# Packing eight heads of 48 into three full blocks of 128 rows instead of four padded ones, with the work replanned around it

## The chip, the core and the metric

The kernel runs on one core of one Trainium2 chip. The core has five instruction queues that run beside each other: PE (matmuls and transposes into the eight PSUM banks), DVE (elementwise, reads PSUM and SBUF), ACT (elementwise with functions such as exp and ln, reads PSUM and SBUF), POOL (elementwise, SBUF only here) and SP (issues the loads and stores). Each runs its instructions in the order in which they were written; semaphores hold an instruction until what it needs is done. The metric is the device time of one execution in microseconds (us); the number for a kernel is the median of its runs.

## What is computed

Two stages. The first is a recurrence over 768 tokens with a state of 48x48 for each of 4 batches x 8 heads; the second mixes tokens within a batch.

```python
B, H, S, D = 4, 8, 768, 48
for t in range(S):
    cur = einsum('bhd,bhe->bhde', u * k[t], v[t])
    y[t] = einsum('bhd,bhde->bhe', r[t], state + cur)
    state = w[t][..., None] * state + einsum('bhd,bhe->bhde', k[t], v[t])
x = y.transpose(0, 2, 1, 3).reshape(B, S, 384)
W = einsum('bsd,btd->bst', x @ w_q, x @ w_k) / 8
out = maximum(einsum('bst,btd->bsd', W, x), 0) @ w_out
```

`r`, `k`, `v`, `w` are float32 of 4x8x768x48 (4.7 MB each), the output is 4.7 MB; inside, bfloat16 operands and float32 sums are used.

## The kernel before

The recurrence is done in chunks of 128 tokens: with `L` the running sum of ln w inside a chunk, `RT = r*exp(L)` and `KT = k*exp(-L)`, the scores of a chunk are `KT^T RT` under a triangular mask, and the state carries what lies before the chunk. A unit is 256 tokens (two chunks) of one batch, so there are 12 units (`n`), three in a batch. For each unit the steps are, by their keys in the code:

- loads `wg`, `kg`, `rg`, `vg` (SP); casts to bfloat16 `k16`, `r16`, `v16` (POOL, a few on ACT); `ln` (ACT, L403);
- `cw`: sums of ln w by matmul with a triangular matrix `CM`; `ep`, `en`: the two exponentials (ACT, L444 and L451);
- `kT`, `rT`: transposes on PE, so that the 48 values of a head lie on the rows; `ks`, `qT`, `RT` (DVE) and `KT` (POOL or DVE) read them from PSUM;
- `vp`/`VB`: a matmul with a permutation `PM` puts v into the order of tokens that the transposes give, and a copy takes it to SBUF; `dps`/`dd`/`Vd`: the bonus term with `u`;
- `A`: scores, one matmul for each head; `AM`: mask (DVE, L592); `kb`/`kd`/`sn`/`SB`: next state;
- `yi`, `ya`: output from state and from scores; `X`: sum with `Vd` (DVE, L724); `xt`/`XT`: transpose; `qk`/`QK`: the projections.

After the third unit of a batch come `T`/`TS` (k-projection times x), and for each unit `mx` (PE), `rl` into `MX` (DVE or ACT), `fp` (times `w_out`), `os` (copy to SBUF) and the store.

The 48 values of a head are padded to 64 rows: two heads fill a block of 128 rows, and a chunk has four blocks (`NP`), so `ks`, `qT`, `RT`, `KT` and `en` are 2 x 512 = 1024 columns wide for a unit. A matmul over one head uses a tile of 64 rows of the array; two heads side by side use both.

`k` and `r` are loaded in runs of four tokens (768 bytes, L232) except in unit 0, `w` and `v` in runs of two (384 bytes, L227), and `v` of the last batch by four DMAs in runs of one token (192 bytes, `vw`, L238), which spares that batch `v16` and `vp`. Units 0 and 11 do `ep`, `en`, `RT`, `KT`, `Vd`, `kb`, `kd` by chunk rather than by unit; unit 11 also `X`, `xt`, `XT` and the projections.

What sets the order: the steps are recorded in a plan, and three tables written in the file, `ORDER`, `WAYS` and `BANKS`, say in which order they are issued, on which engine a step with a choice runs (`A` ACT, `D` DVE, `P` POOL; `E`, `e`, `c` for forms of PE work) and in which PSUM bank a result lies. Nothing is scheduled at run time: an engine that waits holds up all that is behind it.

Of the kernel before, what the change touches and what calls it, by code (L numbers as in the profile page):

```python
# [23 lines left out]
class Buf:  # L24
    def __init__(self, kind, tile=None):
        self.kind = kind
        self.tile = tile
        self.filler = None
        self.before = None
        self.bank = None  # L30


class Plan:

    ENGINE = dict(E="E", e="E", c="E", A="A", D="D", d="D", P="P", S="S", T="S", N="N")

# [4 lines left out]
    def add(self, key, ways, fn, after=(), buf=None, reads=(), cols=0, mode=0, behind=None,  # L43
            half=-1, more=None):
        s = dict(key=key, ways=ways, way=ways[0], fn=fn, after=list(after), buf=buf,
                 reads=list(reads), cols=cols, mode=mode, behind=behind, half=half,
                 more=more or {}, i=len(self.steps), fills=False, out=False)
        if buf is not None:
            if buf.filler is None:
                buf.filler = s  # L50
                s["fills"] = True
                if buf.tile is None:
                    self.banks.append(buf)
                elif behind is None and buf.before is not None:
                    s["behind"] = buf.before.filler
            elif behind is None:
                s["behind"] = buf.filler
        self.steps.append(s)
        return s

    def order(self):
# [7 lines left out]
        assert all((way[("yv",) + k[1:]] == "E") == (w == "A") for k, w in way.items() if k[0] == "X")  # L69
# [4 lines left out]
        for i in ORDER:  # L74
            s = self.steps[i]
            assert s["way"] == "N" or all(x["out"] for x in s["after"]), s["key"]
            if s["buf"] is not None and s["buf"].kind == "x":
                s["buf"].kind = "s" if s["way"] == "E" else "w"
            s["out"] = True
            done.append(s)  # L80
# [38 lines left out]
]  # L119
WAYS = (  # L120
    "PPDPPDPPDDDDDDPDTTPDDAAPPDPPPADDDEENDEAAPPDdPADEAEENDEAAAPAPPADEDcNDEDAAAAAAAAPADdPAAEAc"
    "cNDEADPPDdPAAeAcENDeDAPPDPPAAeAENDEAAAAAAAAAPPDPPAAEDEENDEAAPPDdPAAeAEENDEAAPPDPPAAEAcND"
    "EDAAADAAAAPPDPPAEAEcNDeAAPPDPPAeAccNDeDAPPDPPPAPPAENDEDADNDEAADDDDAAAAAADDADNNEEEENEEENE"
    "NENENNNNNNEN"
)
BANKS = [
# [7 lines left out]
]  # L134


WARM = 24


@with_exitstack  # L140
def kernel(
# [24 lines left out]
    HW = H * D2  # L166
    N = B * NU

# [33 lines left out]
    if not WHOLE:  # L202
        del RINGS["vw"]
# [702 lines left out]
```

## Time and profile before

| what | value |
|---|---|
| runs | 101.3, 103.6, 104.62 us; median 103.6 |
| span of the profiled execution, first to last instruction | 101.1 us |
| granted clock of PE over the span | 1.000 |
| bytes moved, share of time the DMA queue of SP was busy | 24.68 MB, 86.9% |
| packets | 45165, of which 31576 under 512 bytes |

No time of its own is recorded for the profiled execution beside its span; the span lies 0.2 us below the fastest of the runs and 2.5 us below their median. In the rows further down, an engine's busy time counts overlapping instructions once, while the mean of a group is of single instructions, so count times mean is a little more than the busy time. Matmul rows have modelled ends; the distance from one start to the next says more than a duration.

### The profile page before, as it was taken

What the parts mean: (1) busy time and instruction counts of PE and PEld (TensorE: products, weight loads), DVE (VectorE), ACT (ScalarE), POOL (GpSimd) and SP (SyncE); (2) the same over time, 40 slices, a digit from 0 to 9 for tenths busy, and PEclk for the clock granted to TensorE, in tenths of its full rate; (3) what the DMA queues carried; (4) which work ended last, traced back from release to release, by engine and by line L of the source; (5) the groups of instructions that cost most, each with busy time, mean ns of one, the idle gap of its engine ahead of it and who ended that gap; (6) DMA issues with size and microseconds to landing.
All of it is one profiled execution on the core that took longest, in us unless ns stands there. A gap on an engine that the chain in (4) does not pass through costs nothing.

```text
span 101.1 us, 4474 instructions
## 1 busy us (share of the span) xinstructions
PE 86.8 (86%) x1906; PEld 63.4 (63%) x1909; DVE 80.5 (80%) x134; ACT 80.9 (80%) x134; POOL 68.8 (68%) x82
## 2 busy tenths in 40 slices
PE   5966984989899888999899988999999998999920
PEld 1334553777597556678577875787877667776500
DVE  5423896899999989889999899999997897565520
ACT  5068975999799699599998999989997995735930
POOL 6858964699937764968899749999995897000000
PEclk9999999999999999999999999999999999999999
DMA  1999998999999999999999799999888831007591
GB/s 26 309 324 346 332 317 227 341 261 274 313 306 240 257 205 244 291 329 341 224 323 287 192 343 301 166 155 250 229 233 310 314 141 67 0 0 303 209 366 69
DMA packets 45165, 24.68 MB, mean 244 GB/s; under 512 B 31576, under 2 KB 43992, under 8 KB 45144
## 3 DMA queue, kind: packets, MB, share of 16 engines
q1 hardware_dynamic: 44984, 24.19, 86.9%
q8 instruction: 15, 0.25, 1.0%
q10 hardware_dynamic: 160, 0.20, 0.6%
q14 instruction: 6, 0.05, 0.2%
HBM read 19.66 MB, written 4.72 MB: 241 GB/s over the span
## 4 chain that ended last, share of the span: by engine, by line
PE 34%; ACT 15%; DMA 13%; DVE 12%; SPq 10%; issue 7%; POOL 4%; DVEq 0%; POOLq 0%; ACTq 0%
PE PS L177 34%; DMA vg<-in_v_dram 7%; DMA kg<-in_k_dram 6%; ACT ep L444 6%; SPq L227 5%; ACT en L451 4%; SPq L232 4%; DVE AM L592 3%; DVE X L724 2%; ACT os L275 2%; POOL v L281 2%; DVE ks L281 1%; POOL r L414 1%; DVE RT L513 1%; DVE qT L503 1%
## 5 line engine op out<-in xcount | busy, mean ns | idle before, releaser
L592 DVE TENSOR_TENSOR AM<-PS,US 128x1024 bf16<-128x1024 f32 x24 | 28.7, 1216 | 0.9 <-PE PS L177 0.6
L523 POOL TENSOR_TENSOR KT<-ks,en 128x1024 bf16<-128x1024 bf16 (+1 forms) x10 | 17.4, 1739 | 2.7 <-DVE qT L503 2.0
L572 POOL TENSOR_TENSOR Vd<-VB,dd 128x768 bf16<-128x768 bf16 (+1 forms) x14 | 18.0, 1292 | 1.5 <-ACT dd L275 1.0
L444 ACT ACTIVATE ep<-PS,kp 128x512 bf16<-128x512 f32 (+1 forms) x28 | 16.3, 646 | 0.1
L451 ACT ACTIVATE en<-PS,km 128x1024 bf16<-128x1024 f32 (+1 forms) x14 | 13.9, 1002 | 1.1 <-ACT QK L275 0.8
L724 DVE TENSOR_TENSOR X<-PS,Vd 128x768 bf16<-128x768 f32 (+1 forms) x13 | 11.6, 889 | 2.7 <-POOL Vd L572 1.4
L177 PE MATMUL PS<-wo,MX 128*128 128x384 bf16 x72 | 13.3, 326 | 0.2 <-ACT ep L444 0.2
L177 PEld LDWEIGHTS <-KT 48*128 48x128 bf16 (+1 forms) x312 | 10.3, 94 | 5.1 <-issue 2.6
L177 PE MATMUL PS<-RT,KT 48*128 48x128 bf16 x192 | 9.6, 217 | 1.9 <-POOL KT L523 1.0
L414 POOL CAST k<-kg 128x768 bf16<-128x768 f32 x10 | 8.2, 824 | 3.6 <-DMA kg<-in_k_dram 1.8
L281 DVE COPY ks<-PS 128x1024 bf16<-128x1024 bf16 x11 | 7.6, 689 | 3.7 <-PE PS L177 3.7
L275 ACT COPY os<-PS 128x768 f32<-128x768 f32 (+1 forms) x13 | 8.8, 679 | 1.9 <-PE PS L177 1.6
L414 POOL CAST r<-rg 128x768 bf16<-128x768 f32 x10 | 8.2, 824 | 3.1 <-DMA rg<-in_r_dram 1.9
L513 DVE TENSOR_TENSOR RT<-PS,ep 128x1024 bf16<-128x1024 bf16 (+1 forms) x14 | 8.5, 608 | 2.2 <-ACT ep L444 2.0
L403 ACT ACTIVATE lw<-wg 128x768 bf16<-128x768 f32 x12 | 10.1, 850 | 0.1
L177 PEld LDWEIGHTS <-MX 128*128 128x128 bf16 x72 | 6.4, 97 | 4.3 <-DVE MX L289 0.3
L287 ACT ACTIVATE MX<-PS 128x768 bf16<-128x768 f32 (+1 forms) x11 | 8.2, 758 | 0.9 <-PE PS L177 0.8
L275 ACT CAST VB<-PS 128x768 bf16<-128x768 f32 x9 | 7.3, 806 | 1.8 <-PE PS L177 1.7
L281 POOL CAST v<-vg 128x768 bf16<-128x768 f32 x9 | 7.4, 823 | 1.8 <-DMA vg<-in_v_dram 1.7
L177 PE MATMUL PS<-CM,lw 64*128 64x128 bf16 x192 | 7.9, 217 | 0.7 <-issue 0.4
L656 DVE TENSOR_TENSOR SB<-PS,ep 128x192 bf16<-128x192 f32 x20 | 7.0, 350 | 1.6 <-PE PS L177 1.5
L503 DVE TENSOR_TENSOR qT<-PS,ks 128x1024 bf16<-128x1024 bf16 x12 | 8.2, 681 | 0.0
(82 smaller groups left out, 182.8 us busy)
## 6 DMA issues: line engine op xcount, KB each, us to landing
kg<-in_k_dram SPq DMA_DIRECT2D x12, 384.0 KB, 5.5
wg<-in_w_dram SPq DMA_DIRECT2D x12, 384.0 KB, 6.3
rg<-in_r_dram SPq DMA_DIRECT2D x12, 384.0 KB, 6.4
vg<-in_v_dram SPq DMA_DIRECT2D x9, 384.0 KB, 6.9
out_dram<-os SPq DMA_DIRECT2D x9, 384.0 KB, 3.2
vw<-in_v_dram SPq DMA_DIRECT2D x4, 288.0 KB
out_dram<-os SPq DMA_DIRECT2D x5, 192.0 KB, 2.8
wof<-in_moe_w_out_dram SPq DMA_DIRECT2D x1, 450.0 KB
```

Source lines behind the costliest of these rows:

```text
L177: return nc.tensor.matmul(o, l, rr, start=start, stop=stop, skip_group_check=True, is_transpose=trans)
L275: nc.scalar.copy(o, i)
L281: x.tensor_copy(o, i)
L403: nc.scalar.activation(view(lw.tile, 0, [[64, H], [512, 2], [1, D]]), view(g["wg"].tile, 0, [[D2, H], [D, 2], [1, D]]), ACT.Ln, bias=0.0, ...
L414: op(view(o.tile, 0, [[64, NP], [256, 4], [1, D]]), view(g[src].tile, 0, [[2 * D2, NP], [D, 4], [1, D]]))
L444: nc.scalar.activation(view(ep.tile, cs[0] * NP * EW + off, [[EW, NP * len(cs)], [step, 2], [1, 32]]), view(at(cw), cs[0] * 512 + j * 64, ...
L451: nc.scalar.activation(en.tile[:, ds(cs[0] * 512, w_)], at(cw)[:, ds(cs[0] * 512, w_)], ACT.Exp, bias=km, scale=-1.0)
L513: nc.vector.tensor_tensor(plain(RT.tile, cs, 32), turned(512, cs, True), plain(ep.tile, cs, EW // 4), ALU.mult)
L523: x.tensor_tensor(KT.tile[:, cols], ks.tile[:, cols], en.tile[:, cols], ALU.mult)
L572: (nc.vector if e == "D" else nc.gpsimd).tensor_tensor(Vd.tile[:, cols], VB.tile[:, cols], view(dd.tile, cs[0] * H, [[1, len(cs) * H], [0, ...
L592: AMs[c] = add(("AM", n, c), "D", lambda e, c=c, A=A: nc.vector.tensor_tensor(view(AM[c].tile, 0, [[C, 8], [1, C]]), view(at(A), 0, [[C, 8 ...
L724: nc.vector.tensor_tensor(o, y_, view(Vd.tile, c0 * DM, dims), ALU.add)
```

## The change

Each head's 48 values are cut into 32 and 16. Block 0 holds the 32 of the even heads (four strips of 32 rows), block 2 the 32 of the odd heads, and block 1 in each strip the 16 of an even and the 16 of the odd head beside it. A chunk has three full blocks (`G`) instead of four, and `ks`, `qT`, `KT`, `en` and the data of `RT` are 768 columns wide for a unit instead of 1024. Scores and state products of a head become two accumulated matmuls on tiles of 32 rows (`HEADS`). [...]

```diff
+    G = DM // 128
+    R = D2 // G
-    LONG = tuple(range(1, N))
-    WHOLE = (B - 1,)
+    DIRECT = ()
...
         def f_ln(e):
-            nc.scalar.activation(view(lw.tile, 0, [[64, H], [512, 2], [1, D]]),
-                                 view(g["wg"].tile, 0, [[D2, H], [D, 2], [1, D]]), ACT.Ln,
-                                 bias=0.0, scale=1.0)
+            for o, x in blocks(lw.tile, g["wg"].tile):
+                nc.scalar.activation(o, x, ACT.Ln, bias=0.0, scale=1.0)
...
+        def blocks(o, x):
+            return ((view(o, 0, [[R, NP], [C, 4], [1, R]]),
+                     view(x, 0, [[2 * D2, NP], [D, 4], [1, R]])),
+                    (view(o, 4 * C, [[R // 2, H], [C, 2], [1, R // 2]]),
+                     view(x, R, [[D2, H], [D, 2], [1, R // 2]])))
...
+        eps = add(("ep", n), "A", lambda e: nc.scalar.activation(
+            view(ep.tile, 1, [[EC, 2], [EW, G], [1, C]]),
+            view(at(cw), 0, [[512, 2], [C, G], [1, C]]), ACT.Exp, bias=kp, scale=1.0),
...
+        RTs = add(("RT", n), "D", lambda e: nc.vector.tensor_tensor(
+            view(RT.tile, 0, [[512, 2], [1, DM]]), turned(0),
+            view(ep.tile, 65, [[EW, 2 * G], [-65, 2], [1, 64]]), ALU.mult),
+            [rTs, eps] + fresh("ep"), RT, [kr, ep])
+        def f_RM(e):
+            o, x = (view(RT.tile, y * C, [[512, 2], [1, C]]) for y in (3, 1))
+            if e == "A":
+                nc.scalar.activation(o, x, ACT.Copy, bias=0.0, scale=pm)
+            else:
+                on(e).tensor_scalar_mul(o, x, pm)
+        RMs = add(("RM", n), "PDA", f_RM, [RTs, su["pm"]], RT, [])
...
+        HEADS = (((0, 0, 0, R), (1, 1, 1, R // 2)), ((1, 3, 2, R), (2, 2, 3, R)))
+        As = [wide(), wide()]
-            def f_A(e, c=c, A=A):
-                x = at(A)
-                for hp in range(NP):
-                    for hh in range(2):
-                        mm(x[:, ds(hh * 512 + hp * C, C)],
-                           KT.tile[ds(hh * 64, D), ds((c * NP + hp) * C, C)],
-                           RT.tile[ds(hh * 64, D), ds((c * NP + hp) * C, C)])
+        def f_A(e):
+            for c in pair:
+                for hh in range(2):
+                    for y, (kx, rx, _, n_) in enumerate(HEADS[hh]):
+                        for hp in range(NP):
+                            p = ds(hp * R, n_)
+                            mm(at(As[hp // 2])[:, ds(hp % 2 * 512 + c * 256 + hh * C, C)],
+                               KT.tile[p, ds(c * DM + kx * C, C)],
+                               RT.tile[p, ds(c * 512 + rx * C, C)],
+                               start=(c == 0 and hh == 0 and y == 0), stop=(y == 1))
```

`A` is now one step of 32 matmuls for both chunks of a unit and fills four banks at once; `AM` is split by heads, not by chunk. The output `y` of a unit likewise lies in four banks (`ys = [wide(), wide()]`, two before) and `X` is two passes of 384 columns instead of one of 768. `ln` and the casts of `k` and `r` are two instructions each, `ep` is one instead of two. The next state (`sn`) is written by matmuls into 32 rows at a time. In the build, PE has 2229 matmuls where it had 1909.

All four inputs are loaded by `load` in runs of two tokens (384 bytes); `load_long` and `load_whole` are gone, so the last batch has `v16`, `vp` and `VB` like the others. The treatment of units 0 and 11 by chunk is gone but for `rl`, `fp` and `os` of the last batch. The rings `ep`, `RT`, `KT` and `VB` have three buffers instead of two, `os` nine instead of four. The weights are loaded in one DMA each instead of two. `ORDER`, `WAYS` and `BANKS` are new throughout; a few values of `ORDER` read

```diff
-    38, 15, 441, 301, 32, 18, 649, 644, 22, 539, 645, 2, 3, 26, 25, 0, 401, 581, 4, 5, 34, 33, 23,
+    24, 25, 26, 27, 114, 68, 69, 70, 115, 71, 116, 2, 7, 8, 0, 16, 4, 6, 5, 15, 1, 3, 30, 21,
```

What the tables do shows at three places. The first is DVE at the start of the program, from its first read of transposed data on (`X` and `Vd` of the first units stand further down). Before:

```order
L281 COPY ks_95<-PS 128x1024
L513 TENSOR_TENSOR RT_99<-PS,ep_91 128x512
L503 TENSOR_TENSOR qT_97<-PS,ks_95 128x1024
L513 TENSOR_TENSOR RT_99<-PS,ep_91 128x512
L592 TENSOR_TENSOR AM_0_111<-PS,US 128x1024
L283 TENSOR_SCALAR kd_83<-PS 128x8x48
L281 COPY ks_96<-PS 128x1024
L281 COPY dd_107<-PS 128x16
```

and after:

```order
L480 TENSOR_TENSOR KT_108<-PS,en_99 128x768
L290 MEMSET US 128x128
L290 MEMSET ep_96 128x6
L465 TENSOR_TENSOR RT_105<-PS,ep_96 128x2x384
L475 TENSOR_SCALAR RT_105<-RT_105,pm 128x2x128
L461 TENSOR_TENSOR qT_103<-PS,ks_101 128x768
L540 TENSOR_TENSOR AM_0_120<-PS,US 128x1024
L273 COPY UB<-PS 128x24
L290 MEMSET ep_97 128x6
L540 TENSOR_TENSOR AM_0_122<-PS,US 128x1024
```

`RT` of unit 0 was in two halves and is whole, `RM` (the TENSOR_SCALAR with `pm`) follows it, and both masks of unit 0 stand close together; `ks` of unit 0 has gone to ACT.

The second is DVE at the end, from the last mask on. Before:

```order
L592 TENSOR_TENSOR AM_1_114<-PS,US 128x1024
L724 TENSOR_TENSOR X_126<-PS,Vd_110 128x384 x2
L281 COPY os_81<-PS 128x768
L281 COPY XT_120<-PS 128x384
L281 CAST QK_128<-PS 128x128 x2
L281 CAST TS_130<-PS 128x384
L289 TENSOR_SCALAR MX_122<-PS 128x3x128 x2
L289 TENSOR_SCALAR MX_124<-PS 128x3x128 x2
L281 COPY os_82<-PS 128x384
```

and after:

```order
L540 TENSOR_TENSOR AM_1_123<-PS,US 128x1024
L646 TENSOR_TENSOR X_135<-PS,Vd_118 128x2x192
L646 TENSOR_TENSOR X_135<-PS,Vd_119 128x2x192 x2
L646 TENSOR_TENSOR X_135<-PS,Vd_118 128x2x192
L273 COPY XT_129<-PS 128x768
L281 TENSOR_SCALAR MX_130<-PS 128x768
L273 CAST QK_137<-PS 128x384 x2
L273 CAST TS_139<-PS 128x384
L273 COPY os_86<-PS 128x768
L281 TENSOR_SCALAR MX_132<-PS 128x3x128 x2
L273 COPY os_80<-PS 128x384
L273 COPY os_79<-PS 128x384 x2
```

Units 10 (`Vd_118`) and 11 (`Vd_119`) now end side by side: their four passes of `X` and both projections `QK` come behind the last mask, where before only those of unit 11 did; of the last copies `os`, DVE has three instead of one.

The third is SP where the loads end and the stores begin. Before (`vw` is v of the last batch):

```order
L232 DMA kg_73<-in_k_dram 128x4x192
L227 DMA wg_65<-in_w_dram 128x8x96
L232 DMA rg_69<-in_r_dram 128x4x192
L238 DMA vw_131<-in_v_dram 32x48x48 x4
L849 DMA out_dram<-os_79 128x768
L227 DMA wg_66<-in_w_dram 128x8x96
L232 DMA kg_74<-in_k_dram 128x4x192
L232 DMA rg_70<-in_r_dram 128x4x192
L849 DMA out_dram<-os_80 128x768
```

and after:

```order
L228 DMA kg_73<-in_k_dram 128x8x96
L228 DMA rg_69<-in_r_dram 128x8x96
L228 DMA kg_74<-in_k_dram 128x8x96
L228 DMA rg_70<-in_r_dram 128x8x96
L228 DMA vg_77<-in_v_dram 128x8x96
L228 DMA vg_78<-in_v_dram 128x8x96
L739 DMA out_dram<-os_83 128x768
L739 DMA out_dram<-os_81 128x768
```

The four loads of `vw` are gone, and no store stands ahead of a load any more: the first store comes behind the last load.

More of the change, by code (lines that the diff above doesn't have):

```diff
@@ L41, in __init__, with add @@
         self.banks = []
[L43 to L57, printed above, removed]
+    def add(self, key, ways, fn, after=(), fills=(), reads=(), cols=0, more=None):
+        fills = list(fills) if isinstance(fills, (list, tuple)) else [fills]
+        s = dict(key=key, ways=ways, way=ways[0], fn=fn, after=list(after), fills=fills,
+                 reads=list(reads), cols=cols, more=more or {}, i=len(self.steps), out=False)
+        for b in fills:
+            if b.filler is None:
+                b.filler = s
+                if b.tile is None:
+                    self.banks.append(b)
         self.steps.append(s)
@@ L75, in order @@
             s = self.steps[i]
-            assert s["way"] == "N" or all(x["out"] for x in s["after"]), s["key"]
-            if s["buf"] is not None and s["buf"].kind == "x":
-                s["buf"].kind = "s" if s["way"] == "E" else "w"
+            after = s["after"] + s["more"].get(s["way"], ([], []))[0]
+            assert s["way"] == "N" or all(x["out"] for x in after), s["key"]
+            for b in s["fills"]:
+                if b.kind == "x":
+                    b.kind = "s" if s["way"] == "E" else "w"
             s["out"] = True
@@ L382, in unit, with fresh @@
         end = n == N - 1
[L383 to L387 removed]
+        direct = n in DIRECT
+        pair = (0, 1)
+        def fresh(kind):
+            x = used[kind] - 1
+            return [su[kind + str(x)]] if x < RINGS[kind][0] else []
         g = {}
[L390 to L391 removed]
+        for name, ap in (("wg", w), ("kg", k), ("rg", r), ("vg", v)):
+            f = load_rows if name == "vg" and direct else load
@@ L392, in unit @@
             g[name] = ring(name)
-            g[name + "L"] = dma((name, n), lambda e, ap=ap, f=f, x=g[name].tile: f(b, i, x, ap, e),
-                                buf=g[name])
-        if whole and i == 0:
-            batch["vw"] = ring("vw")
-            batch["vwL"] = [dma(("vw", n, q), lambda e, q=q, x=batch["vw"].tile:
-                                load_whole(b, q, x), buf=batch["vw"]) for q in range(4)]
+            g[name + "L"] = dma((name, n), lambda e, ap=ap, f=f, x=g[name].tile: f(b, i, x, ap),
+                                fills=g[name])
@@ L556, in unit @@
         dps, dd = bank(), ring("dd")
         def f_dps(e):
[L559 to L563 removed]
+            for c in pair:
+                for x in range(G):
+                    mm(at(dps)[:, ds(c * H, H)], qT.tile[:, ds(c * DM + x * C, C)],
+                       UB[:, ds(x * H, H)], start=(c == 0 and x == 0), stop=(x == G - 1))
@@ L667, in f_yi @@
-        def f_yi(e, c, start):
-            heads = [(hp, hh) for hp in range(NP) for hh in range(2)]
-            if end:
-                heads.sort(key=lambda x: x[1])
-            for x, (hp, hh) in enumerate(heads):
-                if end and x == NP:
-                    nc.tensor.drain()
-                mm(of(c, 2 * hp + hh), RT.tile[ds(hh * 64, D), ds((c * NP + hp) * C, C)],
-                   olds[c].tile[ds(hh * 64, D), ds(hp * D, D)],
-                   start=(start and hp == 0 and not (end and hh)), stop=False)
@@ L792, in unit @@
-            batch["x"] += [xs] * nc_
+            for kt in range(NK):
+                mm(at(qk)[:, ds(0, U)], wq_sb[:, ds(kt * C, C)], XT.tile[:, ds(kt * U, U)],
+                   start=False, stop=(kt == NK - 1))
+        qs = add(("qk", n), "E", f_qk, [XTs, wts["qk"]], qk, [XT])
+        x = add(("QK", n), "AD", lambda e: copy(
+            e, QK.tile[:, ds(i * QS, QS)], at(qk)[:, ds(0, QS)]), [qs], QK, [qk], cols=384)
+        batch["k"].append(x)
+        batch["x"].append(xs)
         if not final:
```

683 lines of the change are left out of this document (272 added, 411 removed), and 82 rows, old and new, of tables (BANKS, ORDER).

## The prediction

> **What bounds the kernel now.** I read the shares of busy time and the forty slices first, then the busy times by stage, the chain that ended last, and last the prices of the groups. From the page of before:
>
> ```profile
> PE 86.8 (86%) x1906; PEld 63.4 (63%) x1909; DVE 80.5 (80%) x134; ACT 80.9 (80%) x134; POOL 68.8 (68%) x82
> PE   5966984989899888999899988999999998999920
> DVE  5423896899999989889999899999997897565520
> ACT  5068975999799699599998999989997995735930
> GB/s 26 309 324 346 332 317 227 341 261 274 313 306 240 257 205 244 291 329 341 224 323 287 192 343 301 166 155 250 229 233 310 314 141 67 0 0 303 209 366 69
> HBM read 19.66 MB, written 4.72 MB: 241 GB/s over the span
> ```
>
> Three engines are about equally loaded, so no single one is the bound everywhere. The busy times by stage (PE, PEld, DVE, ACT, POOL) separate them:
>
> ```profile
> 10.00:20.00 10.00, 7.80 (x187) 5.77 (x191) 8.50 (x17) 8.27 (x13) 7.07 (x9) 1.00 1.07 303
> 20.00:40.00 20.00, 17.86 (x473) 13.68 (x469) 19.47 (x31) 18.53 (x30) 14.77 (x15) 1.00 1.07 262
> 45.00:65.00 20.00, 18.53 (x490) 14.68 (x490) 19.14 (x29) 19.28 (x31) 16.76 (x16) 1.00 1.05 279
> 65.00:85.00 20.00, 19.36 (x477) 15.17 (x479) 18.32 (x27) 17.92 (x33) 17.41 (x16) 1.00 0.80 220
> 85.00:93.00 8.00, 7.84 (x104) 5.59 (x103) 4.78 (x9) 4.44 (x9) 0.92 (x2) 1.00 0.19 72
> 93.00:101.10 8.10, 3.72 (x24) 1.99 (x22) 2.51 (x5) 3.69 (x8) 0.00 (x0) 1.00 0.61 224
> ```
>
> From 20 to 65 us DVE and ACT are the fullest (DVE 19.47 of 20); from 65 on PE is (19.36 of 20), and from 85 on DVE and ACT stand idle nearly half the time. The chain that ended last says the same: loads in the fill, PE at the end.
>
> ```profile
> 9.04 7.40 DMA vg<-in_v_dram
> 16.49 0.82 POOL v L281
> ...
> 70.60 7.99 PE PS L177 x175
> ...
> 87.56 5.42 PE PS L177 x57
> ```
>
> Four places in the order of time carry the terms below: the first `X`, the loads of `vw`, the last cast of r, and the last mask and last copy.
>
> ```profile
> 18.13 0.96 DVE L724 TENSOR_TENSOR X<-PS,Vd 128x768 bf16<-128x768 f32 x1 [0.99 <-POOL Vd L572]
> 59.67 7.64 SPq L238 DMA_DIRECT2D vw<-in_v_dram  x4
> 77.90 0.83 POOL L414 CAST r<-rg 128x768 bf16<-128x768 f32 x1 [0.66 <-DMA rg<-in_r_dram]
> 85.42 1.22 DVE L592 TENSOR_TENSOR AM<-PS,US 128x1024 bf16<-128x1024 f32 x1
> 96.88 0.56 DVE L281 COPY os<-PS 128x384 f32<-128x384 f32 x1 [1.86 <-ACT os L275]
> ```
>
> **The elementwise engines.** Prices, from the groups by shape:
>
> ```profile
> L592 DVE TENSOR_TENSOR AM<-PS,US 128x1024 bf16<-128x1024 f32 x24 | 28.7, 1216 | 0.9 <-PE PS L177 0.6
> L513 DVE TENSOR_TENSOR RT<-PS,ep 128x1024 bf16<-128x1024 bf16 x10 | 6.8, 683 | 0.2 <-PE PS L177 0.2
> L513 DVE TENSOR_TENSOR RT<-PS,ep 128x512 bf16<-128x512 bf16 x4 | 1.7, 419 | 2.0 <-ACT ep L444 2.0
> L281 DVE COPY XT<-PS 128x768 bf16<-128x768 bf16 x4 | 2.2, 552 | 0.1
> L724 DVE TENSOR_TENSOR X<-PS,Vd 128x768 bf16<-128x768 f32 x11 | 10.5, 950 | 1.6 <-POOL Vd L572 1.4
> L724 DVE TENSOR_TENSOR X<-PS,Vd 128x384 bf16<-128x384 f32 x2 | 1.1, 552 | 1.1 <-PE PS L177 1.1
> L444 ACT ACTIVATE ep<-PS,kp 128x512 bf16<-128x512 f32 (+1 forms) x28 | 16.3, 646 | 0.1
> L451 ACT ACTIVATE en<-PS,km 128x1024 bf16<-128x1024 f32 x10 | 11.3, 1126 | 0.8 <-ACT QK L275 0.8
> L451 ACT ACTIVATE en<-PS,km 128x512 bf16<-128x512 f32 x4 | 2.6, 690 | 0.3 <-PE PS L177 0.3
> L403 ACT ACTIVATE lw<-wg 128x768 bf16<-128x768 f32 x12 | 10.1, 850 | 0.1
> L275 ACT CAST VB<-PS 128x768 bf16<-128x768 f32 x9 | 7.3, 806 | 1.8 <-PE PS L177 1.7
> L523 POOL TENSOR_TENSOR KT<-ks,en 128x1024 bf16<-128x1024 bf16 (+1 forms) x10 | 17.4, 1739 | 2.7 <-DVE qT L503 2.0
> L414 POOL CAST k<-kg 128x768 bf16<-128x768 f32 x10 | 8.2, 824 | 3.6 <-DMA kg<-in_k_dram 1.8
> ```
>
> On DVE a bfloat16 pass of 1024 columns costs 0.68 us and of 512 0.42, so one of 768 costs 0.55 (the copy of 768 shows it). Saved, `ks` and `qT` at the price of `RT`: `ks` 11 x 0.68 to 10 x 0.55, 2.0; `qT` 12 x 0.13, 1.6; `RT` 8.5 to 12 x 0.55, 1.9; `X` 11.6 to 19 x 0.55, 1.1 (the other five of 24 go to ACT). That is 6.6. The mask keeps its 1024 columns: nothing saved on the dearest group. Added, since the new table of engines moves copies here: `os` one pass of 768 and two of 384 more, 2.1; `MX` 3 x 0.95 and 2 x 0.55 for 4 x 0.55, 1.8; `QK`, `TS`, `dd`, `kd` about 2.8; `RM` three passes of 256 columns at 0.25 (under the 0.42 of 512), 0.8. That is 7.5. DVE stays where it is; I take 0, with -0.5 and +1 as ends.
>
> On ACT a pass of 1024 costs 1.13 and of 512 0.69: 0.85 ns a column and 0.25 fixed, so 768 cost 0.91. `ep` 18.1 to 10.9 and `en` 14.0 to 10.9 save 10.3. `lw` in two pieces costs the fixed part twice, 12 x 0.25 = 3.0; `VB` of the last batch 3 x 0.81 = 2.4; five casts of v 4.1; five `X` 2.9; four `RM` 1.9; casts of k and r 1.5: 15.8. What went to DVE takes off about 5.9. Sum -0.4; I take 0. POOL loses 6 to 8 us of `KT` (17.4 less seven passes at 1.3 to 1.6, three quarters of the mean or of a whole pass) and 4 of casts of v, and gains 21 second pieces of casts and five `RM` (0.2 to 0.4 each, the ends being a fixed part as on ACT and half a cast): about -5. It is the emptiest of the four, so this is worth nothing by itself. The body therefore gains nothing: the quarter fewer columns are paid back in moved copies, split casts and the last batch's `VB`.
>
> **PE.** From the order of time, starts of bursts that follow each other without a wait:
>
> ```profile
> 63.94 0.41 PE L177 MATMUL PS<-PM,k 64*128 64x64 bf16 x16
> 64.18 0.40 PE L177 MATMUL PS<-PM,r 64*128 64x64 bf16 x16
> ...
> 75.33 0.56 PE L177 MATMUL PS<-VB,AM 128*128 128x48 bf16 x16
> 75.83 0.40 PE L177 MATMUL PS<-RT,KT 48*128 48x128 bf16 x8
> 76.06 0.27 PE L177 MATMUL PS<-SB,RT 48*128 48x48 bf16 x8
> 76.27 1.15 PE L177 MATMUL PS<-wo,MX 128*128 128x384 bf16 x6
> ```
>
> Sixteen 64-row transposes take 0.24 us, 15 ns each; eight score matmuls 0.23, 29 ns each, two heads abreast. Where the tile's shape changes (75.33 to 75.83 and 76.06 to 76.27) some 0.1 us is left over after sixteen at 25 ns and eight at 14: I take 0.1 for a change of shape. Along PE's order these rise from 123 to 150: +2.7. Scores: 384 matmuls, four strips abreast, half of 29 ns each: as before, 5.6. State products 160 to 320 at 14: +2.2. Transposes of k and r 384 to 288: -1.4; `cw` 192 to 144 at 29: -1.4; `dps`, `kb`, `xt` and the warming matmuls (20 to 13) about -3.2; `yv` and `vp` +1.3. Sum +0.2: PE as full as before. Ends: -2 if the strips overlap so that the state products cost 7, and the rival below.
>
> [...]
>
> **Loads.** `vw` held SP for 7.64 us, and the slices it fills (26th and 27th) move 166 and 155 GB/s; with 384-byte runs almost alone, the 2nd to 6th move 309 to 346. The change takes the 192-byte runs away and turns the 768-byte ones into 384. At 300 GB/s 19.66 MB take 66 us, and the last r is cast at 77.9: cover of about 10 us. So nothing is won or lost; the cover is gone below 265 GB/s, and each 10 GB/s under that costs about 3 us. No load waits behind a store any more; the stores wait, and the slices around 88 us move nothing, so this is hidden.
>
> **Fill.** The first `X` stood 0.99 us because POOL's cast of the second unit's v, waiting for its load, came ahead of `Vd`. In the new order v of unit 0 is the fourth load, not the seventh, and that cast is ACT's. DVE was idle 1.5 us from 10 to 20. I take -1.0, ends -1.5 and +1.0 (the first unit no longer by chunk: `ep`, `en`, `RT` whole and `RM` before the first mask).
>
> **Drain.** From the end of the last mask (86.64) to that of the last copy (97.44) are 10.8 us, in which DVE works 5.7 (4.78 and 2.51 of the last two stages, less 1.6 for the mask itself and a state pass of 0.35 ahead of it). Behind the last mask now stand 14 passes, 9.1 by the prices above or some 8.6 without their overlaps: 3 more, gone from before the mask. The drain itself grows, as two more `X` and the wait for both units' transposes stand before the last projections: +1.4. Net -1.6; ends -3 and 0.
>
> Sum: 0 - 1.0 - 1.6 = -2.6 on the span of 101.1, 98.5. The median of the runs lies 2.5 above the span; I put the change on the median: 103.6 - 2.6 = 101.0.
>
> **Rivals.** First, PE sets the second half (19.36 of 20), so taking DVE work from before the mask does not bring the mask forward by more than PE's work behind it grows (about 2, my estimate for nine `mx` and fifteen projections more behind the last `ya`); the drain then gives -0.6 at most, and with the fill at its forecast or at nothing the time is 102.0 to 103.6: no change.
>
> Second, slower: PSUM. `A` fills four of eight banks at once and `y` holds four until both `X` are done, so `A` of the next unit cannot start until both masks (2 x 1.22 us) of the last are through, and DVE may have nothing to do meanwhile. In before an `A` needs two banks and idle time ahead of the mask is 0.9 us in all. If each of 12 units loses 0.6 us, the time is 101.0 + 7.2 = 108.2; from 0.4 us a unit it is slower by over 2%. For it: the banks; against it: the order puts other DVE work between, and `ep`, `RT`, `KT`, `VB` have a third buffer.
>
> Third, small matmuls at 25 ns: scores 9.6, state products 8.0, together 7.5 more (5.6 and 4.5 now). Before 65 us PE has a tenth free and takes about 2 of it; the rest counts: 106.5. Against it, the 15 ns above.
>
> [...]
>
> **Chances.** Forecast 0.43; no change 0.27; PSUM 0.17; small matmuls 0.07; odd offset 0.06. A measurement of this kernel can tell about 2% from no change, so faster 0.43, within 2% 0.27, slower 0.30. The forecast's own range is 98.5 to 102. The good ends of the four terms together (-0.5, -2, -1.5, -3) would give 96.6, so the range begins at 97; it ends at 106, which holds the first and fourth rivals and the second up to 0.4 us a unit.
>
> **What would show it.** In the changed profile: `RT` near 0.55 and `ep`, `en` near 0.9; 32 scores in some 0.5 us; DVE and ACT within 2 us of 80; the first `X` before 17.5; the last mask's end at 82 to 84 and 12 us from there to the last copy. Waits of PE on DVE's masks before `A`, or of DVE on PE's scores, of several us in total would prove the second rival; 0.8 us or more for 32 scores the third; loads that end after 78 would make the loads the bound.

## The result, and the profile after

The changed kernel takes 109.8 us (median of four runs, 109.4 to 110.9) against 102.9 for the kernel before beside it on the chip: the ratio is 1.080 [1.068, 1.092], slower. The ratios here and all times in the sections below are of a kernel's undisturbed executions, those within 1.5% of its fastest (the expectations go by the medians of all), and the table below leaves out runs whose profiled execution was not one of these. Each ratio is to the kernel before in the same set of runs; its median went from 101.6 to 102.8 us between the sets, so the difference of a time from 109.8 is good to about 1 us. The profiled execution took 109.5 us with a span of 107.8; the one before had a span of 101.1. In every execution the time is 1.7 to 1.9 us above the span.

From the page of the changed kernel:

```profile
PE 91.6 (85%) x2229; PEld 65.1 (60%) x2229; DVE 80.0 (74%) x145; ACT 80.3 (75%) x133; POOL 63.5 (59%) x92
...
PE   5955698789987989887998979999998999999930
...
DVE  2007857567779996989996999998999889873820
...
PEclk9998555555999999999999999999999999999995
```

DVE, ACT and POOL have the totals that were forecast. Two things were not: DVE has no full slice among the first ten, and the clock of TensorE (PEclk, in tenths) is at half from the fifth to the tenth slice, 10 to 27 us. The busy times in steps of 5 us (PE, PEld, DVE, ACT, POOL, clock, DMA share, GB/s), first of the kernel before:

```profile
0.00:5.00 5.00, 3.77 (x9) 1.35 (x10) 2.52 (x13) 1.28 (x1) 3.79 (x19) 1.00 0.64 166
...
10.00:15.00 5.00, 4.25 (x81) 2.90 (x82) 4.72 (x10) 4.39 (x8) 4.13 (x5) 1.00 1.15 325
15.00:20.00 5.00, 3.54 (x109) 2.87 (x109) 3.78 (x8) 3.88 (x6) 2.94 (x5) 1.00 0.98 282
20.00:25.00 5.00, 4.62 (x126) 3.58 (x120) 4.87 (x10) 5.00 (x8) 5.00 (x5) 1.00 1.15 271
25.00:30.00 5.00, 4.54 (x125) 3.63 (x124) 5.00 (x9) 4.45 (x8) 3.40 (x4) 1.00 1.03 305
```

and of the changed one:

```profile
0.00:5.00 5.00, 3.76 (x9) 1.34 (x10) 0.60 (x4) 1.97 (x3) 1.85 (x11) 1.00 0.61 166
...
10.00:15.00 5.00, 3.61 (x78) 2.43 (x77) 4.06 (x9) 3.78 (x7) 2.57 (x5) 0.50 1.16 319
15.00:20.00 5.00, 4.49 (x112) 3.40 (x108) 2.87 (x6) 3.67 (x6) 3.08 (x5) 0.50 0.82 213
20.00:25.00 5.00, 4.08 (x81) 2.59 (x73) 3.58 (x6) 2.44 (x4) 3.12 (x5) 0.50 1.02 276
25.00:30.00 5.00, 4.86 (x139) 3.69 (x140) 3.78 (x8) 2.90 (x6) 3.70 (x7) 0.81 1.03 263
```

From 10 to 30 us DVE works 14.3 us where it worked 18.4. Three moments measure the whole: the end of the third unit's masks, the start of the last mask, the last copy. In the order of time of the changed kernel:

```profile
28.33 2.36 DVE L540 TENSOR_TENSOR AM<-PS,US 128x1024 bf16<-128x1024 f32 x2 [0.76 <-ACT dd L267]
...
90.39 1.22 DVE L540 TENSOR_TENSOR AM<-PS,US 128x1024 bf16<-128x1024 f32 x1
...
103.40 0.56 DVE L273 COPY os<-PS 128x384 f32<-128x384 f32 x1 [0.86 <-PE PS L179]
```

and the one of the kernel before that the prediction does not show:

```profile
26.97 1.21 DVE L592 TENSOR_TENSOR AM<-PS,US 128x1024 bf16<-128x1024 f32 x1
```

I call the time up to the third masks' end the fill (28.18 before, 30.69 now), from there to the start of the last mask the body (57.24 and 59.70), and the rest the end (15.68 and 17.41). The 6.7 us of the spans are 2.5 + 2.5 + 1.7: a part of the loss in each. All later runs are read in these three numbers, each taken from the same rows of its own trace. The last column says how long the clock was at half in the fill and in the body, from windows of 1 us (twice what the granted clock lacks to 1.00):

| kernel | fill | body | end | span | half clock, fill and body |
|---|---|---|---|---|---|
| before | 28.18 | 57.24 | 15.68 | 101.1 | 0, 0 |
| changed | 30.69 | 59.70 | 17.41 | 107.8 | 17.1, 0 |
| e2, before without spread warming matmuls | 29.21 | 56.03 | 15.66 | 100.9 | 10.2, 0 |
| e3, RM from POOL to DVE | 30.94 | 64.00 | 16.96 | 111.9 | 20.5, 6.8 |
| e5, no RM | 29.07 | 59.09 | 17.34 | 105.5 | 17.1, 0 |
| e6, one product | 29.24 | 59.61 | 17.35 | 106.2 | 17.1, 3.4 |
| e7, fewer loads of v | 30.67 | 59.55 | 17.38 | 107.6 | 20.5, 0 |
| e8, two strips at a time | 30.96 | 62.91 | 17.43 | 111.3 | 22.8, 4.5 |
| e11, warm, no RM, one product | 27.10 | 58.51 | 17.99 | 103.6 | 0, 0 |
| e12, RM from DVE to ACT | 34.23 | 59.50 | 17.37 | 111.1 | 23.7, 0.2 |
| e14, masked copy read last | 30.27 | 59.95 | 17.38 | 107.6 | 17.1, 0 |
| e15, three mends | 27.94 | 59.67 | 17.49 | 105.1 | 0, 0 |
| e16, less on DVE | 30.59 | 59.02 | 17.39 | 107.0 | 20.5, 0 |
| e18, less on ACT | 30.89 | 60.04 | 17.37 | 108.3 | 17.1, 0 |

### The profile page after: what moved, and what is told of

Read it like the earlier page. It is cut to its first block, busy times and chain, and to the rows that moved or that the text cites. A ratio compares the mean times of both kernels' runs of the same rounds, so it can differ in the third digit from the quotient of the medians.

```text
span 107.8 us, 5127 instructions
## 1 busy us (share of the span) xinstructions
PE 91.6 (85%) x2229; PEld 65.1 (60%) x2229; DVE 80.0 (74%) x145; ACT 80.3 (75%) x133; POOL 63.5 (59%) x92
## 4 chain that ended last, share of the span: by engine, by line
PE 44%; DVE 27%; POOL 10%; issue 8%; ACT 6%; DVEq 0%; POOLq 0%
PE PS L179 44%; DVE AM L540 9%; DVE ks L273 3%; POOL KT L482 3%; DVE RT L465 3%; POOL Vd L516 2%; DVE qT L461 2%; DVE X L646 2%; DVE SB L590 2%; POOL RT L475 2%; ACT en L434 2%; POOL v L407 1%; DVE os L273 1%; DVE RT L475 1%; DVE KT L480 1%
## 5 line engine op out<-in xcount | busy, mean ns | idle before, releaser
L516 POOL TENSOR_TENSOR Vd<-VB,dd 128x768 bf16<-128x768 bf16 x12 | 17.7, 1477 | 9.7 <-PE PS L179 4.6
L482 POOL TENSOR_TENSOR KT<-ks,en 128x768 bf16<-128x768 bf16 x7 | 11.5, 1640 | 5.0 <-DVE ks L273 2.7
L179 PEld LDWEIGHTS <-KT 32*128 32x128 bf16 (+3 forms) x471 | 10.5, 98 | 4.2 <-issue 2.2
L407 POOL CAST r<-rg 128x512 bf16<-128x512 f32 (+1 forms) x22 | 10.5, 506 | 4.1 <-DMA rg<-in_r_dram 4.1
L403 ACT ACTIVATE lw<-wg 128x512 bf16<-128x512 f32 (+1 forms) x24 | 11.2, 522 | 2.2 <-DMA wg<-in_w_dram 2.2
L430 ACT ACTIVATE ep<-PS,kp 128x768 bf16<-128x768 f32 x12 | 11.0, 917 | 1.7 <-DVE AM L540 1.2
L179 PE MATMUL PS<-RT,KT 32*128 32x128 bf16 (+1 forms) x384 | 10.1, 229 | 1.7 <-DVE RT L465 0.7
L434 ACT ACTIVATE en<-PS,km 128x768 bf16<-128x768 f32 x12 | 10.8, 906 | 0.5 <-PE PS L179 0.3
L646 DVE TENSOR_TENSOR X<-PS,Vd 128x384 bf16<-128x384 f32 x19 | 10.0, 552 | 1.2 <-POOL k L407 0.5
L407 POOL CAST k<-kg 128x512 bf16<-128x512 f32 (+1 forms) x20 | 9.5, 504 | 1.0 <-DMA kg<-in_k_dram 1.0
```

What stands on the lines that cost most here:

```text
L179: return nc.tensor.matmul(o, l, rr, start=start, stop=stop, skip_group_check=True, is_transpose=trans)
L403: nc.scalar.activation(o, x, ACT.Ln, bias=0.0, scale=1.0)
L407: dict(A=nc.scalar.copy, D=nc.vector.tensor_copy, P=nc.gpsimd.tensor_copy)[e](o, x)
L430: eps = add(("ep", n), "A", lambda e: nc.scalar.activation(view(ep.tile, 1, [[EC, 2], [EW, G], [1, C]]), view(at(cw), 0, [[512, 2], [C, G] ...
L434: ens = add(("en", n), "A", lambda e: nc.scalar.activation(view(en.tile, 0, [[DM, 2], [1, DM]]), view(at(cw), 0, [[512, 2], [1, DM]]), ACT ...
L482: nc.gpsimd.tensor_tensor(KT.tile, ks.tile, en.tile, ALU.mult)
```

## The experiments

**The clock.** First theory: the spread warming matmuls of the fill are gone (ten before, one now ahead of 27 us), so the clock falls, and that is the loss. Two runs, one for each direction. In the changed kernel, 17 matmuls on zeros were put ahead of the steps named by number, into PSUM banks that are free there:

```diff
+WARMER = {22: (7, 7, 7, 7), 35: (7,), 50: (7,), 42: (1,), 44: (1, 1, 1), 121: (4,), 54: (2,), 79: (6,), 91: (4,), 94: (1, 1), 100: (0,)}
...
         for s in plan.order():
+            for x in WARMER.get(s["i"], ()):
+                mm(PS[:, ds(x * 512, 512)], Z[:, ds(0, C)], Z)
```

> The changed kernel with 17 more warming matmuls in TensorE's idle gaps of the fill (7 to 24 us). Theory (the granted clock): the clock stays at 1.00 from 5 to 27 us, the first masks of the second and third unit come 2 to 4 us earlier than 20.3 and 28.3 us, and the time falls from 109.8 to 103 to 106 us. Rival (the new step RM, which stands between RT and the scores): the clock may be mended, but the time stays within 1.5 us of 109.8. Rival (the body, after 30 us, is what got slower): a gain of 1 to 2 us, with the 60 us from 30 on as long as before.

107.2 us, ratio 1.051 [1.042, 1.061]: 2.6 us less than the changed kernel, short of the theory's 103 to 106. The clock is at 1.00 all through the fill, and the third masks end 2.3 us earlier (26.06 + 2.36 = 28.42). In the kernel before, the letters of its ten spread `z` steps were set to N:

> The kernel before, without the ten warming matmuls that stand spread between 6.9 and 19.5 us; the ten of its start are kept. Theory (the granted clock): the clock falls to 0.5 somewhere between 8 and 15 us and the time rises from 103 to 106 to 110 us. Rival (the change's new work made the loss): the time stays at 102 to 104 us, whatever the clock does.

102.5 us, ratio 1.004 [0.999, 1.009]. From the page of that run:

```profile
PEclk9999955559999999999999999999999999999999
```

The clock was at half from about 13 to 23 us, the fill ended 1.0 us later, and the body made it good (56.03). So the clock is a part of the loss in the changed kernel and not all of it; the theory as it stood falls.

**RM.** The step `RM` writes the fourth block of `RT`: block 1 times `pm`, which is zero on the rows of the even heads; the scores of the odd heads read it. Its way was overridden by unit, first from POOL to DVE:

```diff
+RM_WAYS = "DDDAADDDAADD"
...
+            if s["key"][0] == "RM":
+                s["way"] = RM_WAYS[s["key"][1]]
             s["eng"] = self.ENGINE[s["way"]]
```

> The changed kernel with the five RM steps of POOL (0.92 us each) moved to VectorE at their places in the order (0.27 to 0.6 us there). Rival (RM is the new wait on the path): 2 to 4 us less than 109.8, since each POOL step of 0.92 us and its two hand-overs go. Theory (the granted clock): within 1.5 us of 109.8, the clock still 0.5 from 10 to 27 us.

114.4 us, 1.120 [1.112, 1.129]: neither theory, 4.6 us worse, nearly all of it in the body. Two rows of DVE there

```profile
50.25 0.94 DVE L479 TENSOR_SCALAR RT<-RT,pm 128x256 bf16<-128x256 bf16 x1
...
54.13 1.23 DVE L479 TENSOR_SCALAR RT<-RT,pm 128x256 bf16<-128x256 bf16 x1
```

and the clock from the page of that run

```profile
PEclk9996555555799999999557999999999999999999
```

show the place. Scores on PE wait 1.83 us for the first of these RM, until 51.24, and from 53.4 to 60.2 us the clock is at half once more. The masks that start at 50.00 in the changed kernel start at 51.86, and the passes of `X` that start at 55.82 there start at 60.29: by then the whole loss is made. What the waits took of it and what the clock took is not told apart. Then RM was left out (`HEADS` reads block 1 for block 3, `f_RM` returns at once):

> The changed kernel without the step RM: the scores read the unmasked block 1 of RT where they read the masked copy, so the masked copy is left out. Theory (three things together: about 4 us of DVE work less done in the fill, 1.5 us more of TensorE work, RM's time on VectorE and in the chain): 2 to 4 us less than 109.8, since RM stands between RT and the scores in every unit and three of its twelve are on VectorE. Rival (TensorE's small matmuls set the body): within 1 us of 109.8.

108.1 us, 1.055 [1.039, 1.070]: 1.7 us less. The fill is 1.6 shorter and the body 0.6. Then with `RM_WAYS = "APAAAPPAAAPP"`:

> The changed kernel with the three RM steps of VectorE (0.28 to 0.82 us, 1.8 us in all) done by ACT at their places in the order; the five of POOL stay. Theory (VectorE's work is paid one for one in the body): 1 to 2 us less than 109.8. Rival (what costs is RM's place in the chain, on whatever engine): within 0.7 us of 109.8.

112.8 us, 1.096 [1.089, 1.104], slower by 3.0 though DVE works 1.7 us less. ACT's rows of that run say why:

```profile
10.68 1.75 ACT L407 ACTIVATE lw<-wg 128x512 bf16<-128x512 f32 x4
12.33 0.49 ACT L477 ACTIVATE RT<-RT,pm 128x256 bf16<-128x256 bf16 x1
```

The first unit's RM now stands behind `lw` of two later units in ACT's queue, and the first mask starts at 13.80 instead of 11.72. Of the 3.3 us that the span grew, the fill has 3.5 and the body none: the 2.1 us of the first unit are paid in full, and the clock stays at half 6.6 us longer.

**Small matmuls, loads, banks.** Three more that each take away one thing or move it:

```diff
-                    for y, (kx, rx, _, n_) in enumerate(HEADS[hh]):
+                    for y, (kx, rx, _, n_) in enumerate(HEADS[hh][:1]):
```

(and the same in `yi`; with `stop=True` in the scores)

> The changed kernel with only the first of the two accumulated products of each score and of each product of the state with RT: 16 matmuls less per unit in the scores and 16 less in the state products, so half of each sum is left out. By the trace 32 scores take 0.77 us a unit and 32 state products 0.6. Rival (TensorE's small matmuls set the body): TensorE does 7 to 8 us less and the time falls by 4 us or more. Theory (dependences between VectorE, POOL and TensorE): it falls by 1 to 3 us.

107.9 us, 1.053 [1.039, 1.068]: 1.9 us less, though PE's busy time fell by 3.4, from 91.6 to 88.2. Nearly all of the gain is in the fill; in the body the clock was at half once more, for 3.4 us.

```diff
+            skip = name == "vg" and n >= 4
-            g[name + "L"] = dma((name, n), lambda e, ap=ap, f=f, x=g[name].tile: f(b, i, x, ap),
+            g[name + "L"] = dma((name, n), lambda e, ap=ap, f=f, x=g[name].tile, skip=skip: skip or f(b, i, x, ap),
```

> The changed kernel without the loads of v from the fifth unit on (its tiles keep the rows of an earlier unit), 3.1 MB of 19.7 MB. If the loads, at 384 and 512 bytes a run and near 320 GB/s at best, hold the body back: 2 to 5 us less than 109.8. Theory (no wait for a load shows behind 15 us): within 1 us of 109.8.

109.8 us, 1.073 [1.060, 1.086]: nothing. The loads of v do not hold the changed kernel.

```diff
-            for c in pair:
-                for hh in range(2):
+            for q, c, hh in [(q, c, hh) for q in range(2) for c in pair for hh in range(2)]:
...
-                        for hp in range(NP):
+                        for hp in (2 * q, 2 * q + 1):
```

> The changed kernel with the 32 scores in another order: first all 16 of the first two strips of 32 rows, then those of the other two, so that the first mask has its two banks after 16 matmuls. If the price of a score is set by how many strips work side by side: above 30 ns each in place of 17 to 24, TensorE 2 to 5 us more and the time up by 1 to 4 us. If the wait for four banks at once is what costs: 1 to 3 us less than 109.8. If the distance is a floor of about 25 ns for any small matmul: the same price and a time within 1 us.

112.9 us, 1.103 [1.091, 1.115]: 3.1 more, in the body. Three neighbouring bursts give the price (start, busy; the next burst's start ends it), of the changed kernel, of e8, and of e6:

```profile
84.99 0.71 PE L179 MATMUL PS<-RT,KT 32*128 32x128 bf16 x32
85.63 0.35 PE L179 MATMUL PS<-ID,X 64*128 64x64 bf16 x12
```

```profile
88.14 0.88 PE L179 MATMUL PS<-RT,KT 32*128 32x128 bf16 x32
88.95 0.35 PE L179 MATMUL PS<-ID,X 64*128 64x64 bf16 x12
```

```profile
86.54 0.40 PE L179 MATMUL PS<-RT,KT 32*128 32x128 bf16 x16
```

Thirty-two scores on four strips take 0.64 us (0.56 in the shortest bursts), on two strips 0.81, and sixteen on four strips about 0.4 (by the row's own duration, whose end is modelled): 20, 25 and 25 ns each. With 0.17 us more a unit, the nine units of the body cost 1.5 us more; the body grew by 3.2, and its clock was at half for 4.5 us where the changed kernel has none. That the first mask had its banks after 16 scores won nothing that shows, so nothing here speaks for the wait for four banks; a gain smaller than these losses would be hidden.

**What the kernel before had.** Its k and r in two-token runs (`LONG = ()`):

> The kernel before with k and r loaded in two-token runs of 512 bytes for every unit, where it had 1024-byte runs from the second unit on. If the shorter runs alone cost something: 1 to 3 us more than 103, with loads that end later than before. Theory (the loads have about 10 us of cover, and the clock is what fell): within 1 us of 103.

103.2 us, 1.017 [1.010, 1.025]: in the kernel before, the long runs were worth about 1.7 us. (They are runs of 768 bytes cut to 384; the expectation's 1024 and 512 bytes are wrong.) Then its first unit, and its last, with `ep`, `en`, `RT` and `KT` done whole in the step of the first chunk (`UNSPLIT` is `(0,)` in e9 and `(11,)` in e10):

```diff
+        def span(cs):
+            return cs if n not in UNSPLIT or len(cs) > 1 else ((0, 1), ())[cs[0]]
...
-            def f_RT(e, cs=cs):
+            def f_RT(e, cs=span(cs)):
+                if not cs:
+                    return
```

> The kernel before with ep, en, RT and KT of the first unit done whole, as the change does them, in place of chunk by chunk; all else as before. Theory (VectorE is the bound from 20 us on, and every microsecond it stands idle in the fill is paid): the first mask comes 1 to 2 us later than 11.1 us and the time rises by 1 to 2 us. Rival (the fill has slack): within 0.5 us of 102.9.

102.4 us, 0.997 [0.991, 1.003]: no difference that can be told.

> The kernel before with ep, en, RT and KT of the last unit done whole in place of chunk by chunk. Theory (in the change the time from the last mask's end to the last copy grew from 10.8 to 12.3 us since the last unit is no longer done in pieces, and its mask comes later too): 0.5 to 1.5 us more than 102.9. Rival (TensorE sets the end, 19.4 of 20 us busy from 65 us on): within 0.4 us.

101.9 us, 0.993 [0.987, 0.998]: no loss, if anything a gain of 0.7%. In the kernel before, these four steps can be done whole at either end without a loss; that this holds in the changed kernel's order too is not shown.

**Do the parts add?** The edits of e1, e5 and e6 in one kernel:

> The changed kernel with the fill's extra warming matmuls, without RM and with one product in place of two (the masked copy and half of each sum of the scores and state products are left out): the three edits that alone gave 1.7, 1.4 and 1.1 us less. Theory (the loss is a sum of small parts, each paid through VectorE): they add, 105 to 106 us. If they hide one another, as with one wait behind all three: 107 to 108.5 us. If they were each hidden by the others: 103 us or less.

104.8 us, 1.020 [1.009, 1.031]: 5.0 less, for 2.6 + 1.7 + 1.9 = 6.2 apart; the fill is 3.6 shorter, for 2.3 + 1.6 + 1.4 = 5.3 apart. They add in the main, and by these numbers overlap by 1 to 2 us. Its last mask starts at 85.61, as before the change (85.42); what is left of the span's difference stands behind it.

**Mends that keep the result.** The first is `ks` of the first unit on DVE, the second turns the loops over `c` and `hh` in `f_A` around, the third has both and e1's warming matmuls:

> The changed kernel with one copy moved: ks of the first unit by VectorE, which stands idle until 8.4 us there, in place of ACT. Theory (a delay of the first unit's chain is paid one for one up to the last mask, as the run with RM on ACT showed in the other direction): RT starts 0.4 to 0.8 us earlier than 9.46 us, the first mask ends that much earlier, and the time falls by 0.4 to 0.8 us. Rival (later waits swallow it): less than 0.3 us.

109.4 us, 1.071 [1.062, 1.081]: inconclusive. The first mask started 0.8 us earlier (10.91), and no gain of time can be told.

> The changed kernel with the scores of heads 0 (both chunks) before those of heads 1, so that 16 of the 32 are issued before the masked copy is read, in place of 8. Theory (RM costs 1.4 us through its place ahead of the scores): 0.3 to 1 us less than 109.8. Rival (RM costs only its engines' time): within 0.3 us.

109.3 us, 1.072 [1.065, 1.079]: 0.5 us less, the fill 0.4 shorter; too little to be told from nothing.

> The changed kernel with three mends that keep its result: the warming matmuls in the fill, ks of the first unit on VectorE, and the scores of heads 0 first. Theory (small parts of the fill and of RM add up): 106 to 107.5 us, 2.5 to 4 less than 109.8, and still 3 or more above the kernel before, since the second products and the longer end remain. If one wait hides behind the others: 107.5 to 108.5. If the fill was all of the loss: below 104.

106.8 us, 1.051 [1.043, 1.058]: 3.0 less, clear of the changed kernel's interval. In the order of time of e15:

```profile
25.58 2.36 DVE L544 TENSOR_TENSOR AM<-PS,US 128x1024 bf16<-128x1024 f32 x2 [0.61 <-PE PS L183]
...
87.61 1.22 DVE L544 TENSOR_TENSOR AM<-PS,US 128x1024 bf16<-128x1024 f32 x1
```

The third masks come 2.75 us earlier than in the changed kernel and the last 2.78: the two kernels run parallel from 28 us on. It is the best of the changed kernels that compute the whole result, and still slower than the kernel before; no changed kernel here beats that.

**The body.** Its busy times (PE, PEld, DVE, ACT, POOL), of the kernel before and of the changed one:

```profile
28.18:85.42 57.24, 53.44 (x1336) 41.76 (x1336) 53.20 (x78) 52.29 (x88) 45.80 (x43) 1.00 0.95 252
```

```profile
30.69:90.39 59.70, 54.68 (x1595) 41.13 (x1595) 53.58 (x95) 53.59 (x90) 46.22 (x56) 1.00 0.83 233
```

Three runs took work off one engine each: half of one mask in units 3 to 9 (`nb_ = 4` blocks of columns for 8), the last of three products of the projection in the first three batches (`range(NK - 1)`), the second piece of `lw` from unit 3 on (`blocks(...)[:1]`).

> The changed kernel with the second mask of units 3 to 9 over 512 of its 1024 columns (the other half is left out): some 4 us less on VectorE, all of it in the body (from the end of the third unit's masks to the start of the last mask, 59.7 us in the changed kernel against 57.2 before). If VectorE sets the body: it shortens by 2.5 to 4 us and the time falls to 106 to 107.3. If another engine does, or dependences do: by less than 1 us.

108.8 us (of two executions, without an interval) beside 101.6 for the kernel before in that set, with DVE's busy time 3.5 us less: the body is 0.7 shorter and the time about 1.0.

> The changed kernel without the last of the three products of the output projection in the first three batches (a third of each sum is left out): 18 matmuls of 128x384, at 0.17 us each 3.1 us less on TensorE, nearly all in the body. If TensorE sets the body: it shortens by 2 to 3 us and the time falls to 106.8 to 108. If another engine does: by less than 1 us.

108.1 us, 1.062 [1.052, 1.072]: about 1.7 less for 3.1 us of matmuls, as the expectation prices them. Its profiled execution ran at 0.558 of the clock over its span (last section), so its body can't be read.

> The changed kernel without the second piece of lw from the fourth unit on (its tile keeps the rows of an earlier unit): 9 passes of 0.41 us, 3.7 us less on ACT in the body. If ACT sets the body: it shortens by 2 to 3.7 us and the time falls to 106 to 108. If another engine does: by less than 1 us.

109.5 us, 1.076 [1.067, 1.085], with ACT 2.3 us less: nothing that can be told.

So none of the three engines, each near 90% full, sets the body alone, since none is paid one for one: of PE's work about half is paid, of DVE's less than a third. The changed kernel's own runs spread over 1.5 us, so that PE comes first is likely and not shown. e8, where dearer matmuls are part of a longer body, fits; e6, where PE did 1.4 us less in the body and it stayed at 59.6, cannot decide, since its clock was at half for 3.4 us of it.

## Why the prediction was wrong, step by step

**The elementwise engines (0).** The prices were right: `RT` 554 ns where 0.55 was forecast, `ep` 917, `en` 906. From the groups of the changed kernel:

```profile
L465 DVE TENSOR_TENSOR RT<-PS,ep 128x768 bf16<-128x768 bf16 x12 | 6.6, 554 | 0.9 <-PE PS L179 0.9
...
L475 POOL TENSOR_SCALAR RT<-RT,pm 128x256 bf16<-128x256 bf16 x5 | 4.6, 924 | 5.0 <-DVE RT L465 4.4 <-PE PS L179 0.6
```

Two sizes were off. RM costs 0.92 on POOL (forecast 0.2 to 0.4) and 0.59 in the mean on DVE (0.25), and it stands between `RT` and the scores: e5 gives 1.7 us for the whole step, where the sum had it as work alone. And the total of DVE hid a difference: the kernel before spent 2.52 us of its 80.5 before 5 us, on constants and pads, while nothing else could run; the changed one spends 0.60. The work that counts is therefore 78.0 and 79.4, 1.4 us more and not 0.

**PE (+0.2).** The scores were taken at 0.5 us a unit and cost 0.56 to 0.72 in most units, 0.87 and 0.96 in two. In the body PE is busy 1.2 us more and idle 1.2 us more (57.24 - 53.44 = 3.80, 59.70 - 54.68 = 5.02), together the 2.5 that it lengthened. The warming matmuls entered this term as a saving, "20 to 13", and no term asked what the clock would do without them. That is one failed step, worth 2.6 us by e1.

**Loads (0).** Right for the changed kernel, as far as e7 shows. Everything else is later in it, which may be why the cover was there; in the kernel before the same runs of k and r cost 1.7 (e4).

**Fill (-1.0, ends -1.5 and +1.0).** It is +2.5, so this step failed by 3.5 us. The first `X`, which was to start before 17.5, starts at 18.68 (18.13 before). The forecast saw that one wait would go and left out what comes in: RM ahead of the first scores, twice as many of them at half clock, and `ks` of the first unit in ACT's queue behind `en`. With the clock held and RM and the second products left out (e11) it ends at 27.1, with the three mends (e15) at 27.9, against 28.2 before: what the forecast expected of the new order was there, and RM, the second products and the clock took it back.

**Drain (-1.6).** One half was right: from the end of the last mask to that of the last copy it is 12.35 us (103.96 - 91.61), forecast 12. The other half is the largest failed step: passes gone from before the mask should have brought it forward by 3, and the body is 2.5 longer instead, 5.5 off. DVE does have 2.5 us more to do from the last mask on:

```profile
90.39:107.80 17.41, 12.74 (x183) 8.43 (x174) 9.55 (x17) 7.57 (x13) 0.00 (x0) 0.93 0.43 160
```

against

```profile
85.42:101.10 15.68, 11.14 (x114) 7.22 (x112) 7.01 (x14) 7.71 (x16) 0.50 (x1) 1.00 0.41 153
```

but what it has less of before that mask lies in the fill (80.5 - 53.2 - 7.0 = 20.3 us before, 80.0 - 53.6 - 9.6 = 16.8 now), where it stands idle nearly half the time; in the body it does 0.4 more. And e16 shows what taking work from DVE in the body is worth: 3.5 us of it made the body 0.7 shorter. The first rival had said that this would not bring the mask forward by as much, and on that point it was right; its price of no change was not, since the fill and RM were not in it.

The three misses, 3.5 in the fill, 5.5 in the body and 0.3 behind the last mask's start (1.7 for 1.4), make the 9.3 us between the -2.6 forecast for the span and the 6.7 measured. The base was 0.7 too high besides: the forecast put 2.5 us between span and time, where every execution has 1.7 to 1.9.

**The rivals.** PSUM: its 108.2 comes nearest to the measured time, by luck, since its mechanism is not there; DVE's masks wait 2.3 us on PE in all, where it needed 7.2, PE waits 0.9 on masks, and e8 eased the banks without a gain that shows. Small matmuls at 25 ns (in the kernel before the price of one in `ya`: eight from 66.57 to 66.77 us): right for e8's two strips, 0.81 us for 32, and wrong for four strips, 0.56 to 0.64 us (17.5 to 20 ns each); where the rival put 5.5 us on them, taking half of them away gave 1.9, nearly all in the fill. Odd offset (0.06 of the chances, and the fourth rival that the range's upper end holds): no run shows that it costs anything; `RT`, which reads `ep` from column 65, took 554 ns, beside 547 for `qT` and 550 for the copy `XT` of as many columns.

What adds up: clock 2.6, RM 1.7, second products 1.9, jointly 5.0 by e11, which puts the fill 1.1 us below that of the kernel before. The end is 1.7 longer, near the forecast's 1.4, by the work placed behind the last mask; that is argued from the rows above and was not tried alone. And 1.3 us of the body stay without a cause that a run has shown: e11 leaves it at 58.5 against 57.2.

## What to carry to other kernels

Where several engines are nine tenths full, a sum of busy times does not give the time: ask of each saved microsecond which engine pays for it, and take setup work in the first microseconds out of the totals first. In the changed kernel a delay in the first units reached the end (e12), and so did a gain (e15), while 3.5 us taken from DVE in the body shortened it by 0.7; in the kernel before, 1.0 us lost in the fill did not reach the end (e2). When a change drops matmuls on zeros (10.2 us at half clock in e2; 2.6 us of the time back in e1), or makes PE wait in the fill (6.6 us more at half in e12), price the clock as a term of its own, and look at it in every stage of a trace before a difference is put down to the edit; and a small step between a product and its consumer costs by its place in the queue, which can be more than its own duration (0.49 us of RM on ACT made the first mask 2.1 later).

## What the hardware showed that was not expected

The clock fell while PE was at work: 0.79 us of the microsecond in which it fell, 1.7 us after an idle of 1.29 (6.91 to 8.20). In steps of one microsecond of the changed kernel (PE busy, clock, DMA share, GB/s):

```profile
7.00:8.00 1.00, 0.00 (x0) 1.00 1.17 323
8.00:9.00 1.00, 0.37 (x3) 1.00 1.16 323
9.00:10.00 1.00, 0.79 (x18) 0.94 1.17 323
10.00:11.00 1.00, 0.61 (x20) 0.50 1.17 325
...
24.00:25.00 1.00, 1.00 (x25) 0.50 0.73 183
25.00:26.00 1.00, 1.00 (x43) 0.50 1.04 278
26.00:27.00 1.00, 1.00 (x19) 0.53 0.98 206
27.00:28.00 1.00, 1.00 (x42) 1.00 1.03 264
```

The time at half clock was a multiple of about 3.4 us wherever the table has a spell whole: 10.2, 17.1 and 20.5 in the fill, 3.4 and 6.8 in the body. In the 3.4 us ahead of the fall at 9.87 PE had worked 1.6; in the body of e6, near 32.5 us, the clock fell after 2.5 us of work in 3.4. In the changed kernel it came back at 26.94, 3.7 us into a stretch without a gap (23.27 to 28.22); the longest such stretch before it in the spell had 3.0 us (13.08 to 16.07), or 3.8 across a gap of 0.03. What decides a fall or a return is not shown.

In one of four executions of e17 the clock stood between 0.5 and 0.6 in every slice from the third on, at 0.558 over the span, and the time was 124.3 us against 107.9 to 108.3 in the other three, whose clock was 0.893 to 0.914:

```profile
PEclk9855555555555555555555555555555555555555
```

In the changed kernel a multiply of 128x256 by a column of scalars took 0.92 us on POOL, 0.51 on ACT and 0.28 to 0.82 on DVE (up to 1.23 in e3), where a cast of 256 columns took POOL 0.40.
